# Pooled attention and a gated conv FFN on one core: conv on two blocks at once, keys of batches 2 to 7 in pairs

## The chip, the core and the metric

The kernel runs on one core of a Trainium2 chip. Its engines work side by side, each through its own list: TensorE (PE, matrix products; its weight loads are shown apart as PEld), VectorE (DVE), ScalarE (ACT), GpSimd (POOL) and SyncE (SP). Products land in PSUM, eight banks of 512 fp32 columns on 128 partitions. The metric is the device time of one execution in microseconds (us).

## The reference

Eight batches of 8 heads, 576 positions, 64 columns a head. Keys and values are averaged over groups of 8 positions (72 remain), softmax attention is computed against those 72, the heads are joined to x (8, 576, 512), and a gated FFN with a conv over positions follows. All inputs and outputs are fp32.

```python
k_p = k.reshape(B, H, Sp, pool, D).mean(axis=3)
v_p = v.reshape(B, H, Sp, pool, D).mean(axis=3)
scores = scale * np.matmul(q, k_p.transpose(0, 1, 3, 2))
attn = softmax(scores)                      # max subtracted first
x = join_heads(np.matmul(attn, v_p))
h = np.maximum(x @ w_in, 0.0)               # 512 -> 1024
conv_out = sum of conv_w[k] * h shifted by k - 1, k = 0..2
out = (h * sigmoid(conv_out)) @ w_out       # 1024 -> 512
```

## The kernel before

**Tiling.** Batches go in groups of two (g = 0 to 3). A group has nine query tiles of 128 rows (tile 4 takes 64 rows of each of its batches). The FFN works per batch on eight blocks `fb` of 128 hidden channels (partitions) by 576 positions, and writes out per tile of 128 rows.

**Keys, queries, values.** POOL loads all three with a cast to bf16 (`load_heads` L352, `load_v` L365). Keys of a batch are pooled on PE: `prep_k` (L464) multiplies each slice by the 0/1 matrix `pm`, which sums eight positions and turns the result at once, in two halves of 18 products with the array split in two (L469) or 36 with it split in four (L479); `copy_k` (L494) takes them out of PSUM. `prep_q` turns queries on PE (L533). `prep_v` adds values three times on DVE (L503, widths 1280, 640, 320) and multiplies them by the head mask into `vm` (L507), whose mask operand is broadcast along its last dimension. Key buffers: a ring `kp` of three, one a batch.

**Attention of a tile.** Scores on PE (L585), maximum on DVE (L598), subtraction (DVE L610 from group 1 on), exp on ACT (L636), a transpose of e (PE L647 in groups 0 and 1, then a DMA on SP's queue, L656), the product with `vm` (L672), division on DVE (L685, L687), and a transpose of x into `xT` (PE L704, or SP's DMA L696 in groups 2 and 3).

**FFN of a batch.** `ffn_in` (L717; batch 0 by tiles, L738) and a relu on ACT (L726) give `hT`. The conv is three products per position run with diagonal matrices `dw`, with the array split into four 64 by 64 parts: row half r, column half c. A part (r, c) with r = c reads `hT`; the parts with r different from c work on the same block with its two channel halves exchanged, which needs the copy `hX` (`ffn_swap`, L783, one DVE or ACT copy per half and pair of blocks). So one `ffn_conv` (L788) fills two banks of one block: row half r makes the positions of half r. Then tanh (ACT L815), plus one (DVE L825), times h (DVE L826) into `gT`, and `ffn_out` (L833, eight products of 512 columns a tile), a copy to `osb` (L844, ring of five) and two stores from SP's queue (L856).

**What sets the order.** `Graph.order` (L97) plans the whole program: every operation has a duration, the buffers it uses and a key (a due time plus a hand-set nudge). Among those that can start now, each engine takes the lowest key; PE's keys get `STAY` off if the array's split stays. `either` operations go to DVE or ACT. At most eight loads are in flight (L194). PSUM tokens take one bank or an aligned pair (`place`, L139). The list is then emitted in order of planned start, and each engine's list runs in that order. `first(name)` (L924) sets the keys of the early loads to -88 plus their place in `early` plus the nudge `('l', name)`.

Of the kernel before, what the change touches and what calls it, by code (L numbers as in the profile page):

```python
# [8 lines left out]
FP32 = mybir.dt.float32  # L9
# [24 lines left out]
class Graph:  # L34
# [8 lines left out]
    STAY = 111.55  # L43
    LAZY = 1.11
# [5 lines left out]
    ATT = 39.8  # L50
    SPREAD = -183.35
    PREP_K = -29.07
    PREP_Q = 51.67
    PREP_V = 749.64
    GATE = 126.95
    CONV = 47.63
    SWAP = 261.14
    QCONV = -325.78
    OUT = 297.24
    LAST = 982.97  # L60
    FIRST = 196.4
    V0 = 281.91
    DW = 1007.11
# [3 lines left out]
    SWAP_DVE = 8  # L67
    BANKS = 8
    URGENT = -857.49
    NUDGE = {  # L70
# [12 lines left out]
    }  # L83

    def __init__(self, rings):
        self.rings, self.ops, self.spares = rings, [], []

# [180 lines left out]
def kernel(  # L268
# [13 lines left out]
    POOL = 8  # L282
# [911 lines left out]
```

## Time and profile before

| What | us |
|---|---|
| median of three runs | 244.89 |
| the runs | 244.22, 244.89, 246.25 |
| span of the profiled execution | 244.0 |
| PE, DVE, ACT, POOL busy | 220.9, 182.0, 168.3, 29.1 |

The profiled execution is shown by its span, from its first to its last instruction; a clocked time of its own is not shown beside it. Its span lies 0.9 below the median and 0.2 below the shortest run.

A line of a group reads: source line, engine, operation, output <- inputs, shapes, count | busy us in total, mean ns of one | idle time of the engine just before, and what ended it. Matmuls are pipelined, so the duration of one is longer than the distance to the next. A line of waits reads: who waited <- for what: us in total, times, longest. In the table by stretch, each engine has its busy us and the number of its instructions in brackets; PEclk is the granted clock of PE as a share of full speed.

### The profile page before, as it was taken

How to read it: one execution, taken by the hardware profiler on the slowest of the kernel's cores; microseconds unless marked ns; L12 is line 12 of the kernel's file. 1: busy time of each engine (PE TensorE's matmuls, PEld its weight loads, DVE VectorE, ACT ScalarE, POOL GpSimd, SP SyncE). 2: the span in 40 equal slices, each digit the busy share in tenths (PEclk: the TensorE clock that was granted, in tenths of full speed). 3: DMA queues.
4: the chain of work that ended last, by engine and by line, in shares of the span. 5: the costliest groups of instructions: out<-in, count | busy, mean ns of one | idle time of the engine just before them, and what ended most of it. 6: DMA issues, size and time to landing. Idle time of an engine off the chain costs nothing.

```text
span 244.0 us, 7852 instructions
## 1 busy us (share of the span) xinstructions
PE 220.9 (91%) x3354; PEld 154.3 (63%) x3377; DVE 182.0 (75%) x398; ACT 168.3 (69%) x264; POOL 29.1 (12%) x48
## 2 busy tenths in 40 slices
PE   6568998998999999999999996979999999899991
PEld 2446986876675676678775554757655576676440
DVE  7667648899999999999999995755799413956301
ACT  2254764599996876498998654949966386989330
POOL 7942223200122020220010000000000000000000
PEclk9999999999999999999999999999999999999998
DMA  5999999999189958697208568593216577400356
GB/s 81 164 205 207 207 208 208 207 207 202 22 141 185 197 83 190 104 179 153 46 3 141 126 134 91 107 139 89 24 46 149 109 137 167 117 3 6 84 137 164
DMA packets 43707, 31.53 MB, mean 129 GB/s; under 512 B 23680, under 2 KB 39064, under 8 KB 43672
## 3 DMA queue, kind: packets, MB, share of 16 engines
q0 software_dynamic: 15952, 16.26, 42.2%
q1 hardware_dynamic: 27640, 14.64, 29.5%
q8 instruction: 26, 0.43, 0.7%
q10 hardware_dynamic: 80, 0.13, 0.2%
q14 instruction: 9, 0.07, 0.1%
HBM read 32.52 MB, written 9.44 MB: 172 GB/s over the span
## 4 chain that ended last, share of the span: by engine, by line
PE 51%; DVE 26%; ACT 8%; DMA 7%; issue 5%; POOL 0%; SPq 0%; DVEq 0%; ACTq 0%; POOLq 0%
PE psum L833 16%; PE psum L717 14%; PE psum L803 7%; DVE negm L598 5%; DVE gT L826 4%; PE psum L672 3%; DVE sd L610 3%; DMA kp<-in_k_dram 3%; PE psum L738 3%; DVE tg L825 2%; ACT hT L726 2%; DVE hX L783 2%; DVE x L687 2%; DVE v L503 2%; DMA eT<-e 2%
## 5 line engine op out<-in xcount | busy, mean ns | idle before, releaser
L833 PE MATMUL psum<-w_out_sb,gT 128*128 128x512 bf16 x266 | 66.6, 379 | 2.0 <-issue 0.8
L717 PE MATMUL psum<-xT,w_in_sb 128*128 128x288 bf16 x448 | 61.1, 286 | 2.0 <-DMA xT<-x 1.3
L717 PEld LDWEIGHTS <-w_in_sb 128*128 128x128 bf16 x448 | 41.8, 98 | 15.4 <-DMA xT<-x 1.6
L833 PEld LDWEIGHTS <-gT 128*128 128x128 bf16 x288 | 26.0, 98 | 25.9 <-issue 0.7
L815 ACT ACTIVATE tg<-psum 128x576 bf16<-128x576 f32 x64 | 37.8, 655 | 3.0 <-PE psum L803 2.5
L726 ACT ACTIVATE hT<-psum 128x576 bf16<-128x576 f32 x56 | 34.4, 648 | 7.5 <-PE psum L717 7.1
L844 ACT COPY osb<-psum 128x512 f32<-128x512 f32 (+1 forms) x31 | 17.9, 579 | 24.5 <-PE psum L833 23.3
L783 DVE COPY hX<-hT 64x1152 bf16<-64x1152 bf16 x41 | 18.7, 458 | 18.3 <-ACT hT L726 15.4
L803 PE MATMUL psum<-hT,dw 64*64 64x224 bf16 (+3 forms) x576 | 30.9, 246 | 0.8 <-ACT tg L815 0.7
L803 PEld LDWEIGHTS <-dw 64*64 64x64 bf16 x1152 | 24.7, 107 | 10.5 <-issue 9.5
L826 DVE TENSOR_TENSOR gT<-tg,hT 128x576 bf16<-128x576 bf16 x64 | 29.3, 458 | 2.2
L803 PE MATMUL psum<-hX,dw 64*64 64x288 bf16 (+3 forms) x576 | 30.7, 246 | 0.0
L598 DVE TENSOR_REDUCE negm<-psum 128x8 f32<-128x576 f32 (+1 forms) x36 | 25.9, 750 | 2.4 <-PE psum L585 2.2
L783 ACT COPY hX<-hT 64x1152 bf16<-64x1152 bf16 x23 | 26.4, 1150 | 0.5
L687 DVE TENSOR_TENSOR x<-psum,r 128x512 bf16<-128x512 f32 x36 | 24.9, 692 | 1.2
L636 ACT ACTIVATE e<-sd 128x576 bf16<-128x576 f32 x27 | 18.2, 682 | 8.1 <-DVE sd L610 6.7
L672 PE MATMUL psum<-vm,eT 128*128 128x130 bf16 (+5 forms) x240 | 18.5, 222 | 4.2 <-DMA eT<-e 2.2
L825 DVE TENSOR_SCALAR tg<-tg 128x576 bf16<-128x576 bf16 x64 | 19.4, 304 | 3.4 <-ACT tg L815 3.2
L672 PEld LDWEIGHTS <-eT 128*128 128x128 bf16 (+1 forms) x240 | 14.7, 100 | 9.4 <-issue 3.0
L610 DVE TENSOR_TENSOR sd<-psum,negm 128x576 f32<-128x576 f32 x27 | 19.6, 749 | 0.1
L685 DVE RECIPROCAL r<-psum 128x8 f32<-128x8 f32 x36 | 7.3, 201 | 8.8 <-PE psum L672 8.7
L543 ACT COPY qT<-psum 128x1152 bf16<-128x1152 bf16 (+2 forms) x11 | 10.7, 992 | 4.2 <-PE psum L533 4.1
(67 smaller groups left out, 227.9 us busy)
## 6 DMA issues: line engine op xcount, KB each, us to landing
out_dram<-osb SPq DMA_DIRECT2D x71, 128.0 KB, 2.4
v<-in_v_dram POOLq DMA_DIRECT2D x8, 512.0 KB, 8.8
kp<-in_k_dram POOLq DMA_DIRECT2D x7, 576.0 KB, 16.0
qp<-in_q_dram POOLq DMA_DIRECT2D x7, 576.0 KB, 12.5
w_in_sb<-in_moe_w_in_dram POOLq DMA_DIRECT2D x2, 512.0 KB, 14.7
w_out_sb<-in_moe_w_out_dram POOLq DMA_DIRECT2D x1, 1024.0 KB, 20.0
kp<-in_k_dram POOLq DMA_DIRECT2D x2, 288.0 KB, 5.4
v<-in_v_dram POOLq DMA_DIRECT2D x8, 64.0 KB, 8.4
```

Source lines behind the costliest of these rows:

```text
L598: nc.vector.tensor_reduce(out=a["m"][0:rows], in_=a["s"][0:rows, :, 0:2 * KW].rearrange("p a (h s) -> p a h s", s=Sp), axis=AX.X, op=OP.ma ...
L610: nc.vector.tensor_tensor(out=a["d"][0:rows], in0=a["s"][0:rows, :, 0:2 * KW].rearrange("p a (h s) -> p a h s", s=Sp), in1=a["m"][0:rows]. ...
L672: nc.tensor.matmul(out=a["o"][lo:hi, h // 4, (h % 4) * (D + 1):(h % 4 + x1 - x0) * (D + 1)], lhsT=a["eT"][:, j, lo:hi], rhs=buf("vm", b)[: ...
L687: nc.vector.tensor_tensor(out=a["x"][0:rows].rearrange("p (a h d) -> p a h d", a=2, d=D), in0=ov[:, :, :, 0:D], in1=r[0:rows].unsqueeze(3) ...
L717: nc.tensor.matmul(out=banks(ps)[:, j, 0:SC], lhsT=w_in_block(dc, fb), rhs=buf("xT", g)[:, dc, i * S + j * SC:i * S + (j + 1) * SC], start ...
L726: nc.scalar.activation(out=buf("hT", b)[:, fb, :].rearrange("p (a s) -> p a s", a=2), in_=banks(ps)[:, :, 0:SC], func=ACT.Relu, scale=0.5,)
L783: copy(out=buf("hX", b, f2)[r * D:(r + 1) * D, :, :], in_=buf("hT", b)[(1 - r) * D:(2 - r) * D, 2 * f2:2 * f2 + 2, :],)
L803: nc.tensor.matmul(out=cps[c * D:(c + 1) * D, r, lo:hi], lhsT=dw[r * D:(r + 1) * D, int(r != c), tap * n_fb + fb, :], rhs=hT[r * D:(r + 1) ...
L815: nc.scalar.activation(out=tg.rearrange("p (a s) -> p a s", a=2), in_=banks(ps)[:, :, 0:SC], func=ACT.Tanh, scale=0.5,)
L825: nc.vector.tensor_scalar(out=tg, in0=tg, scalar1=1.0, scalar2=None, op0=OP.add)
L826: nc.vector.tensor_tensor(out=buf("gT", g)[:, fb, i * S:(i + 1) * S], in0=tg, in1=buf("hT", b)[:, fb, :], op=OP.mult)
L833: nc.tensor.matmul(out=bank(ps)[0:rows, :], lhsT=buf("gT", g)[:, fb, t * P:t * P + rows], rhs=w_out_sb[:, fb, :], start=(fb == 0), stop=(f ...
```

## The change

Conv works on two neighbouring blocks in one operation. Part (r, c) takes block 2 f2 + (r xor c) straight from `hT`; so the odd block comes out with its channel halves exchanged, and each of the two blocks gets both position halves over two turns. `ffn_swap`, `hX` and the exchanged half of `dw` are gone; the operation takes two pairs of PSUM banks together. The gate of an odd block puts the halves back: two half-height additions of one, from `tg` into `gT`, then the product in place.

Keys of batches 0 and 1 are loaded and pooled as before, into halves of the one buffer `kk` (ring of 1). Those of 2 to 7 come in pairs of batches by one load, each partition holding 72 successive rows; DVE sums them in three additions (`pool_pair`, widths 2304, 1152, 576), PE only turns and sorts them with a selector `pick` (`turn_pair`, 18 products of 64 columns for both batches), and four copies (`copy_pair`) place them in `kT`.

The head mask is widened once into `mask_wide` and the `vm` product reads that. Output tiles of batches 3 to 6 are stored from POOL's queue, the others from SP's as before. The planner learns of two pairs of banks and of stores on POOL, and all keys and nudges are different numbers. The diff, cut to its core:

```diff
...
-    STAY = 111.55
-    LAZY = 1.11
+    STAY = 2433.79
+    LAZY = 9.06
...
+    KPOOL = 273.64
+    KTURN = 389.36
+    PREP_Q = 13123.61
+    CONV = -17463.4
+    QCONV = -11593.41
+    STORE_POOL = (3, 4, 5, 6)
+        ('kk', 1): 4004.89, ('kk', 2): -10943.52, ('kk', 3): 2758.46, ('l', 'ident'): 29827.78, ('l', 'k0'): -18933.08, ('l', 'k0+'): -1804.54,
+        ('l', 'k1'): 8531.98, ('l', 'kk1'): -15453.62, ('l', 'mask'): -5336.49, ('l', 'out'): 16585.15, ('l', 'pm'): 18123.21, ('l', 'q0'): -5392.93,
+        ('l', 'q0+'): -19585.27, ('l', 'q1'): -14428.56, ('l', 'q2'): -14105.83, ('l', 'q3'): -6312.58, ('l', 'v0'): 4052.12, ('l', 'v1'): 20762.22,
+        ('l', 'v2'): -6439.13, ('l', 'w0'): 11766.78, ('l', 'w1'): -7006.96, ('lk', 4): -8391.13, ('lk', 6): -8475.04, ('lq', 4): -6745.14,
...
-                f = place(need)
+                f = place(need) if need <= 2 else two_pairs()
...
+
+        def two_pairs():
+            f = [idle_from(x) for x in banks]
+            c = sorted(max(now, f[i], f[i + 1]) for i in range(0, len(f), 2) if None not in (f[i], f[i + 1]))
+            return c[1:2] or None
...
+                elif e == "POOL":
+                    o.end = max(wire, s + d + 0.3) + fixed
+                    landings += [o.end] * o.dmas
-             "hT": 2, "gT": 2, "xT": 2, "qT": 3, "kp": 3, "qp": 2, "hX": 3, "v": 2, "vm": 5, "kT": 5, "sd": 3, "r": 3, "s": 2}
+             "hT": 2, "gT": 2, "xT": 2, "qT": 3, "kk": 1, "qp": 2, "v": 2, "vm": 5, "kT": 5, "sd": 3, "r": 3, "s": 2}
...
+    mask_wide = const.tile([P, NJ, 3, D], BF16, name="mask_wide")
+    pick = const.tile([P, 2, D], BF16, name="pick")
-    cw_raw = const.tile([3 * n_fb, 3 * D], FP32, name="cw_raw")
-    convw = const.tile([P, 2, 3 * n_fb], FP32, name="convw")
+    cw_raw = const.tile([3 * n_fb, P], FP32, name="cw_raw")
+    convw = const.tile([P, 3 * n_fb], FP32, name="convw")
-    dw = const.tile([P, 2, 3 * n_fb, D], BF16, name="dw")
...
-        "hX": ([P, 2, S], BF16),
...
+    def k_rows_of(b):
+        t = buf("kk", 0).rearrange("p c x -> p (c x)")[:, b * H // 2 * S:(b + 1) * H // 2 * S]
+        return t.rearrange("p (h x) -> p h x", h=H // 2)
...
+    def load_pair(g):
+        rows = k[groups[g][0]:groups[g][1] + 1].rearrange("b h s d -> (b h s) d").rearrange("(p r) d -> p (r d)", p=P)
+        nc.gpsimd.dma_start(out=buf("kk", g).rearrange("p c x -> p (c x)"), in_=rows)
+
...
-        load_heads(buf("kp", b), k, b, **part)
+        load_heads(k_rows_of(b), k, b, **part)
...
-        nc.sync.dma_start(out=cw_raw[:, P:P + D], in_=cw[:, 0:D])
+        nc.sync.dma_start(out=cw_raw, in_=cw)
...
+    def widen_mask():
+        nc.vector.tensor_copy(out=mask_wide, in_=mask.unsqueeze(3).to_broadcast([P, NJ, 3, D]))
+
+    def build_pick():
+        for hh in range(2):
+            for f in range(2):
+                nc.vector.tensor_copy(
+                    out=pick[:, hh].rearrange("p (s f a e) -> p s f a e", s=2, f=2, a=2)[:, :, f],
+                    in_=ident.rearrange("p (s a hh f e) -> p s a hh f e", s=2, a=2, hh=2, f=2)[:, :, :, hh, f],
+                )
+
...
         nc.vector.tensor_tensor(
-            out=dw[:, x, todo],
+            out=dw[:, todo],
             in0=ident_2.unsqueeze(1).to_broadcast([P, n, D]),
-            in1=convw[:, x, todo].unsqueeze(2).to_broadcast([P, n, D]),
+            in1=convw[:, todo].unsqueeze(2).to_broadcast([P, n, D]),
             op=OP.mult,
...
+    def pool_pair(g, step):
+        t, half = buf("kk", g), POOL * D >> step + 1
+        nc.vector.tensor_tensor(out=t[:, :, 0:half], in0=t[:, :, 0:half], in1=t[:, :, half:2 * half], op=OP.add)
+
+    def turn_pair(g, ps):
+        flat = banks(ps).rearrange("p a x -> p (a x)")
+        for c in range(C):
+            for hh in range(2):
+                nc.tensor.matmul(
+                    out=flat[hh * D:(hh + 1) * D, c * D:(c + 1) * D],
+                    lhsT=buf("kk", g)[:, c, 0:D],
+                    rhs=pick[:, hh],
+                    start=True,
+                    stop=True,
+                    skip_group_check=True,
+                )
+
+    def copy_pair(b, ps, hh, copy):
+        g, i = where[b]
+        part = slice(hh * D, (hh + 1) * D)
+        src = banks(ps).rearrange("p a x -> p (a x)")[part, 0:C * D].rearrange("p (c s j e) -> p s j e c", s=2, j=4, e=8)
+        copy(
+            out=buf("kT", b)[part, :, hh * Sp:(hh + 1) * Sp].rearrange("p j (e c) -> p j e c", c=C),
+            in_=src[:, i],
+        )
...
             in0=vt[:, :, 0:D].unsqueeze(2).to_broadcast([P, NJ, 3, D]),
-            in1=mask.unsqueeze(3).to_broadcast([P, NJ, 3, D]),
...
-    def ffn_swap(b, f2, r, copy):
-        copy(
-            out=buf("hX", b, f2)[r * D:(r + 1) * D, :, :],
-            in_=buf("hT", b)[(1 - r) * D:(2 - r) * D, 2 * f2:2 * f2 + 2, :],
-        )
-    def ffn_conv(b, fb, ps):
+    def ffn_conv(b, f2, pss):
         g, i = where[b]
-        hT, hX = buf("hT", b), buf("hX", b, fb // 2)
-        cps = banks(ps)
-        for n in range(max(map(len, todo))):
-            for r in range(2):
-                for c in range(2):
-                    if n >= len(todo[r]):
+        for turn in range(2):
+            for n in range(max(map(len, todo))):
+                for r in range(2):
+                    j = r ^ turn
+                    if n >= len(todo[j]):
                         continue
-                    tap, lo, hi, src = todo[r][n]
-                    nc.tensor.matmul(
-                        out=cps[c * D:(c + 1) * D, r, lo:hi],
-                        lhsT=dw[r * D:(r + 1) * D, int(r != c), tap * n_fb + fb, :],
-                        rhs=hT[r * D:(r + 1) * D, fb, src:src + hi - lo] if r == c
-                        else hX[r * D:(r + 1) * D, fb % 2, src:src + hi - lo],
-                        start=(n == 0),
-                        stop=(n == len(todo[r]) - 1),
-                        skip_group_check=True,
-                    )
+                    tap, lo, hi, src = todo[j][n]
+                    for c in range(2):
+                        fb = 2 * f2 + (r ^ c)
+                        nc.tensor.matmul(
+                            out=banks(pss[r ^ c])[c * D:(c + 1) * D, j, lo:hi],
+                            lhsT=dw[r * D:(r + 1) * D, tap * n_fb + fb, :],
+                            rhs=hT[r * D:(r + 1) * D, fb, src:src + hi - lo],
+                            start=(n == 0),
+                            stop=(n == len(todo[j]) - 1),
+                            skip_group_check=True,
+                        )
 
-            out=buf("gT", g)[:, fb, i * S:(i + 1) * S], in0=tg, in1=buf("hT", b)[:, fb, :], op=OP.mult
-        )
+        tg, gate = buf("tg", b, fb), buf("gT", g)[:, fb, i * S:(i + 1) * S]
+        if fb % 2:
+            for r in range(2):
+                nc.vector.tensor_scalar(
+                    out=gate[r * D:(r + 1) * D], in0=tg[(1 - r) * D:(2 - r) * D], scalar1=1.0, scalar2=None, op0=OP.add
+                )
+            tg = gate
+        else:
+            nc.vector.tensor_scalar(out=tg, in0=tg, scalar1=1.0, scalar2=None, op0=OP.add)
+        nc.vector.tensor_tensor(out=gate, in0=tg, in1=buf("hT", b)[:, fb, :], op=OP.mult)
...
+        if kind == "k":
+            toks[b] = kk.setdefault(0, tokens.get(("kk", 0)) or token("kk", 0))
...
+    def add_load_pair(g, key):
+        kk[g] = token("kk", g)
+        loads["kk", g] = add({"POOL": 0.65}, key, lambda: load_pair(g), uses=[kk[g]], land=(LATE, 2 * kb, RATE))
...
+    def add_pair(g, key):
+        b0 = groups[g][0]
+        prev = None
+        for step, d in enumerate((1.352, 0.752, 0.452)):
+            prev = add(dve(d), key + nudge("kk", g) + Graph.KPOOL + step, lambda step=step: pool_pair(g, step),
+                       after=[prev, loads["kk", g]], uses=[kk[g]])
+        t = token("ps", n=2)
+        for b in groups[g]:
+            ktok[b], kdone[b] = token("kT", b), []
+        o = add({"PE": 0.30}, key + nudge("kk", g) + Graph.KTURN, lambda: turn_pair(g, t), after=[prev, picked],
+                uses=[t, kk[g]], mode=HALF, count=36)
+        for b in groups[g]:
+            for hh in range(2):
+                c = add(either(0.46, 0.42), key + nudge("kk", g) + Graph.KTURN + 1, None, after=[o, zk], uses=[t, ktok[b]])
+                c.emit = lambda c=c, b=b, hh=hh: copy_pair(b, t, hh, copier(c))
+                kdone[b].append(c)
+
...
-        for step, d in enumerate((0.81, 0.49, 0.32, 1.16)):
+        for step, d in enumerate((0.81, 0.49, 0.32, 0.65)):
...
+        for f2 in range(n_fb // 2):
+            fbs = (2 * f2, 2 * f2 + 1)
+            cbs, tgs = [token("ps", n=2) for _ in fbs], [token("tg", b, fb) for fb in fbs]
+            conv = add({"PE": 0.66}, w + 6 * f2 + Graph.QCONV, lambda f2=f2, cbs=cbs: ffn_conv(b, f2, cbs),
+                       after=relu[fbs[0]] + relu[fbs[1]] + dwo, uses=cbs + tgs + [htok[b], gtok[g]], mode=QUARTER, count=64 + 12 * i)
...
-            add({"SP": 1.18}, key, lambda t=t: ffn_store(g, t, nc.sync), after=[o], uses=[osb], land=(2.0, 0, 1))
+            if b in Graph.STORE_POOL:
+                add({"POOL": 1.55}, key, lambda t=t: ffn_store(g, t, nc.gpsimd), after=[o], uses=[osb], land=(2.4, 0, 1)).dmas = 2
+            else:
+                add({"SP": 1.18}, key, lambda t=t: ffn_store(g, t, nc.sync), after=[o], uses=[osb], land=(2.0, 0, 1))
...
```

More of the change, by code (lines that the diff above doesn't have):

```diff
@@ L49 @@
     IN_FLIGHT = 8
[L50 to L63, printed above, removed]
+    ATT = -1794.24
+    SPREAD = -4830.66
+    PREP_K = -4885.51
+    KPOOL = 273.64
+    KTURN = 389.36
+    PREP_Q = 13123.61
+    PREP_V = 12374.2
+    GATE = 153.55
+    CONV = -17463.4
+    QCONV = -11593.41
+    OUT = 10943.62
+    LAST = 8939.04
+    FIRST = 17466.52
+    V0 = -17959.82
+    DW = 14591.19
     X_DMA = 4
@@ L466, in prep_k @@
             for hh in range(2):
-                k_rows = buf("kp", b)[:, 2 * half + hh, c * D:(c + 1) * D]
+                k_rows = k_rows_of(b)[:, 2 * half + hh, c * D:(c + 1) * D]
                 if mode == HALF:
@@ L929 @@
     add_load("k", 0, first("k0+"), 0.5, heads=slice(2, 4))
-    cwl = add({"SP": 1.1}, soon(), load_conv, land=(1.5, 0, 1))
+    cwl = add({"SP": 0.6}, soon(), load_conv, land=(1.5, 0, 1))
     cb0 = add({"DVE": 0.25}, soon(), lambda: nc.vector.memset(blank, 0.0))
@@ L1009, in add_prep_v @@
         prev = None
-        for step, d in enumerate((0.81, 0.49, 0.32, 1.16)):
+        for step, d in enumerate((0.81, 0.49, 0.32, 0.65)):
             prev = add(dve(d), key + step * gap, lambda step=step: prep_v(b, step),
-                       after=[prev, lv[b], hmc], behind=[vdone.get(b - 1)], uses=[vtok[b]] + [vmtok[b]] * (step == 3))
+                       after=[prev, lv[b], hmc, hmw], behind=[vdone.get(b - 1)], uses=[vtok[b]] + [vmtok[b]] * (step == 3))
         vdone[b] = prev
```

89 lines of the change are left out of this document (41 added, 48 removed), and 21 rows, old and new, of the table NUDGE.

## The prediction

> **What bounds the kernel now.** The page first, for the span and the share of each engine; then the chain that ended last.
>
> ```profile
> span 244.0 us, 7852 instructions
> PE 220.9 (91%) x3354; PEld 154.3 (63%) x3377; DVE 182.0 (75%) x398; ACT 168.3 (69%) x264; POOL 29.1 (12%) x48
> PE 51%; DVE 26%; ACT 8%; DMA 7%; issue 5%; POOL 0%; SPq 0%; DVEq 0%; ACTq 0%; POOLq 0%
> ```
>
> TensorE (PE) carries half of the chain, VectorE (DVE) a quarter. Those are averages, so next the table of busy time by stretch:
>
> ```profile
> core 0: us, PE busy (x) PEld busy (x) DVE busy (x) ACT busy (x) POOL busy (x), PEclk, DMA share, GB/s
> 0.00:24.00 24.00, 16.07 (x225) 10.27 (x228) 17.27 (x46) 9.36 (x18) 14.55 (x27) 1.00 1.05 163
> 24.00:48.00 24.00, 22.75 (x473) 20.27 (x468) 16.79 (x34) 14.84 (x22) 6.33 (x9) 1.00 1.23 208
> 48.00:96.00 48.00, 45.63 (x866) 33.19 (x869) 46.58 (x99) 39.52 (x64) 4.82 (x7) 1.00 0.88 156
> 96.00:144.00 48.00, 46.67 (x680) 32.45 (x685) 46.20 (x94) 38.49 (x60) 3.40 (x5) 1.00 0.63 109
> 144.00:168.00 24.00, 20.50 (x247) 14.78 (x246) 14.75 (x34) 15.81 (x26) 0.00 (x0) 1.00 0.73 121
> 168.00:228.00 60.00, 58.38 (x835) 38.59 (x842) 39.28 (x93) 46.99 (x72) 0.00 (x0) 1.00 0.40 81
> 228.00:244.00 16.00, 10.92 (x50) 4.80 (x49) 1.12 (x2) 3.30 (x6) 0.00 (x0) 0.94 0.54 131
> ```
>
> From 48 to 144 us DVE (92.8 of 96) and PE (92.3) are both full; from 168 to 228 PE alone (58.4 of 60). From 24 to 228 us PE stands idle for only 204 - 193.9 = 10.1 us, a third of it in 144 to 168. The granted clock is 1.00 throughout, so no clock gain is open. The gain is therefore limited by what PE no longer has to do, plus part of these 10.1 us. Two of PE's waits there, from the list of waits, and the queue of SyncE (SP) just before, from the timeline:
>
> ```profile
> PE psum L672 <- DMA eT<-e: 2.2, 1, 2.2
> PE psum L717 <- DMA xT<-x: 1.3, 1, 1.3
> ```
>
> ```profile
> 159.38 2.98 SPq L856 DMA_DIRECT2D out_dram<-osb  x4
> 162.45 1.26 SPq L696 DMA_TRANSPOSE xT<-x  x1
> 163.76 2.51 SPq L856 DMA_DIRECT2D out_dram<-osb  x4
> ```
>
> Stores and DMA transposes share SP's queue; a transpose waits behind 3 us of store issues. The prices come from the groups by line and shape:
>
> ```profile
> L826 DVE TENSOR_TENSOR gT<-tg,hT 128x576 bf16<-128x576 bf16 x64 | 29.3, 458 | 2.2
> L783 ACT COPY hX<-hT 64x1152 bf16<-64x1152 bf16 x23 | 26.4, 1150 | 0.5
> L825 DVE TENSOR_SCALAR tg<-tg 128x576 bf16<-128x576 bf16 x64 | 19.4, 304 | 3.4 <-ACT tg L815 3.2
> L783 DVE COPY hX<-hT 64x1152 bf16<-64x1152 bf16 x41 | 18.7, 458 | 18.3 <-ACT hT L726 15.4 <-PE psum L803 2.0
> L507 DVE TENSOR_TENSOR vm<-v,mask 128x960 bf16<-128x960 bf16 x8 | 9.2, 1156 | 0.2
> L469 PE MATMUL psum<-pm,kp 128*64 128x144 bf16 x180 | 8.2, 247 | 3.6 <-DMA kp<-in_k_dram 3.6
> L503 DVE TENSOR_TENSOR v<-v 128x1280 bf16<-128x1280 bf16 x8 | 6.5, 818 | 0.2 <-DMA v<-in_v_dram 0.2
> L503 DVE TENSOR_TENSOR v<-v 128x640 bf16<-128x640 bf16 x8 | 3.9, 489 | 0.2
> L479 PE MATMUL psum<-pm,kp 64*64 64x72 bf16 x216 | 3.0, 197 | 0.0
> ```
>
> **Keys on PE.** The pooling products of batches 2 to 7 go. Restricted to lines 469 and 479, the stretches 20 to 96 us show 1.51 + 4.06 + 1.12 + 1.01 = 7.7 us busy in 12 half-batches. A run's last matmul shows about 0.2 us that the next run overlaps, so 7.7 - 12 x 0.2 = 5.3 leaves the path. Three groups of 18 products over 64 columns are added; the nearest row, 18 transposes of 128 columns (line 533), lasts 0.69 us, so at most 2.1, and half of that by columns. I take 0.8: net -4.5, ends -3.2 (5.3 - 2.1) and -6.7 (7.7 - 1.0). PE is full there, so all of it counts.
>
> **Keys on DVE.** The two rows of line 503 give (818 - 489)/640 = 0.514 ns an element, so 2304, 1152 and 576 elements take 1.34 + 0.75 + 0.46 = 2.55 us a pair, 7.7 us for three. Two pairs fall in 48 to 144. The copies out of PSUM keep their number (12 of 288 elements a partition, 0.39 us on ScalarE (ACT), 0.45 on DVE) and read with a stride: from no change to double, of which I take no change, since one element takes about 1 ns in the other PSUM reads too (692 ns for 512); doubled it is 12 x 0.4 = 5 us on ACT, which has 18 us free in 48 to 144.
>
> **Conv.** Two blocks hold as many products and weight loads as before (two old blocks in a row, 218.44 to 219.39 us, take 0.95 us). A change of tile shape costs 0.11 to 0.14 us at each end; I count 29 separate conv runs now and there can be about 32, so nothing. The copies of h go: 26.4 us of ACT, 18.7 of DVE. Every odd block gets a second half-height addition: 32 x 0.30 = +9.7 us of DVE (between 0.15 and 0.30 each; a 64-partition copy pays by its columns, so the upper end).
>
> **vm product.** Eight at 1.156 us. At the slope of line 503, 960 elements would take 0.65: between 0 and -4.0 us of DVE, and I take -4.0. The Trainium skill, VectorE: DVE Perf Modes, section What auto-detection actually checks, asks 16-bit operands with step one for two results a cycle; the old mask operand stands still along its last dimension, the new one does not, so by the page -4.0. Left at 1.156, DVE keeps 3 us more in 48 to 144, which still does not pass PE, and the total stays.
>
> **DVE and ACT together, 48 to 144 us.** DVE 92.8 - 10.2 (22 hX copies) + 4.9 (16 additions) - 3.0 (six vm) + 5.1 (two key pairs) = 89.6; ACT 78.0 - 11.5 (ten hX copies) = 66.5. ACT can then take half of the 6.6 us of qT, eT and xT copies that DVE makes there: DVE 86. PE: 92.3 less its share of the keys = 89. PE is then the fuller one and this stage can end 3 us earlier by its work alone; that is inside the -4.5.
>
> **Waits.** Of the 10.1 us I take 4: 2 of 3.5 in 144 to 168 (no hX copy between relu and conv, 0.46 to 1.15 us each, and fewer stores in SP's way), 1.5 of 3.7 in 48 to 144, 0.5 elsewhere. Ends: 0 and 10.1.
>
> **Stores.** 18 tiles of batches 3 to 6, 36 issues, leave SP (0.587 each, 21 us) for GpSimd (POOL; a load issue there takes 0.55 to 0.77, so 27 us). POOL is busy 29 us, none after 128. Its queue also holds the loads of batches 4 to 7, which wait up to 18.5 us for a buffer (q7, issued 126.8); a store ordered behind such a load waits too. SP's 14th tile, the first of batch 3 if stored in order, is issued at about 160, so at nothing.
>
> **Start.** The nudges order POOL's loads by key, lowest first: second part of q0, first half of k0, q1, second half of w_in, first part of q0, rest of k0, v0, k1; pm and ident follow only when eight transfers are in flight. So 2.3 MB, counted in bf16, instead of 0.85 MB land before the first scores. At the rates of slices 1 to 3 (81, 164, 205 GB/s) that is about 16 us instead of 11, and v0 19 instead of 13. But k0, both q0, v0, k1, q1 and the weights are the same 5.05 MB, landed at about 29 us in both orders, and PE can turn q1 meanwhile. I take +1.5, ends 0 and +5. One key buffer instead of three: the pair of 2 and 3 can be loaded once batch 1 is pooled (now 20 us), and batch 2 is now pooled at 38 to 41; the median landing of 16 us just fits, at nothing. If it is late, the +5 covers it. The smaller conv tables take two 0.95 us products from DVE, the widened mask and the selector add 0.3 to 1.6, while DVE waits for the first scores: nothing.
>
> **Sum.** 244.0 - 4.5 - 4 + 1.5 = 237.0 us of span. The profiled span is 0.9 below the median of 244.89, so 237.9.
>
> **Rivals.**
> Everything recovered: all 10.1 us, nothing lost at the start. 244.0 - 4.5 - 10.1 + 0.9 = 230.3. Against it: PE and DVE stay within 3 us of each other for 96 us.
> No gain: DVE stays the bound. If ACT takes no copies, vm stays at 1.156 and all three pairs are pooled after 48 us, DVE holds 89.6 + 3.0 + 2.5 = 95.1, above the 92.8 of now; the 2.3 us more and the late start's +1.5 meet the 2 + 0.5 us of waits and 1.4 of keys outside this stage: about 244.8. Against it: ACT has 29 us free there.
> Slower: a conv now needs four of the eight PSUM banks at once and holds the second pair through two tanh (0.24 + 2 x 0.655 us). PE works through one list, in the order planned, so a wait for banks stops it whole. Each of the 32 convs has 7/32 = 0.22 us to lose before the gain is gone. A wait of one tanh (0.655) at every second gives 16 x 0.655 = 10.5: 248.4. For it: the only bank wait of a conv now (0.7 us, on a tanh) already stands in a stretch of four blocks in a row. Against it: tanh starts earlier, ACT being rid of the hX copies.
> Late stores: five output buffers, 1.73 us of PE per tile. A store then costs 1.5 to issue and, at the median landing of v's load, 8.8, plus 0.6 of copy: 10.9/5 = 2.2 us a tile, 0.45 too much, 18 x 0.45 = 8 us: 246. It decides above a landing of 5 x 1.73 - 2.1 = 6.5 us; loads' landings include the queue of other loads, and SP's stores land in 2.4. The Trainium skill, SBUF, State Buffer, section Who interferes with whom, says that GpSimd cannot write descriptors while DVE runs a two-port operation. No slowing shows here: load issues at 66 to 108 us, with DVE full, take the same 0.74 to 0.77 us as at 4 us.
>
> **Chances.** Forecast 0.60 (233 to 242); everything recovered 0.16; no gain 0.08; conv waits for banks 0.11; late stores 0.05. About 1% is what a measurement of this kernel can tell from no change. Faster 0.76 (the first two), same 0.09 (no gain, a little of late stores), slower 0.15. Range 229.5 to 245.5: from all waits recovered and the larger end of the keys, to no gain; the slower cases, 0.14, lie mostly outside.
>
> **What would show it.** Right: no hX; lines 469 and 479 only before about 25 us; odd blocks' additions at 0.30; DVE clearly below PE from 48 to 144; vm at 0.65; store issues on POOL with landings under 6.5 us. Wrong: PE waiting for tanh ahead of conv, copies of osb waiting for stores, first scores later than 17 us without being made up by 48, or strided key copies far above 0.45.

## The result, and the profile after

The changed kernel takes 252.22 us (median of 250.58, 251.78, 252.66 and 252.88); the kernel before, on the same chip, 245.56 (244.22, 244.89, 246.22, 246.25). Ratio 1.029, interval 1.023 to 1.035: slower by about 3%, where 237.9 us and a gain were forecast. The profiled execution of the changed kernel has a span of 248.9 us; its own time, 250.58, is 1.7 more. It is the fastest of the four, so the trace shows 4.9 us of the 6.7 that the medians lie apart. Spans are compared with spans below. Medians and ratios leave out executions over 1.5% above the fastest of the same kernel (one of run 2, two of run 11).

The page of the changed kernel, the lines that answer to those of before:

```profile
span 248.9 us, 7483 instructions
PE 217.9 (88%) x3172; PEld 149.5 (60%) x3194; DVE 175.7 (71%) x396; ACT 148.2 (60%) x246; POOL 45.2 (18%) x81
PE 44%; DVE 26%; issue 10%; DMA 9%; POOL 5%; ACT 5%; DVEq 0%; ACTq 0%; POOLq 0%; SPq 0%
```

PE, DVE and ACT each work less than before: PE by 3.0 us, DVE by 6.3, ACT by 20.1. The span is 4.9 us longer all the same, so PE must stand idle 7.9 us more. The table by stretch shows where:

```profile
core 0: us, PE busy (x) PEld busy (x) DVE busy (x) ACT busy (x) POOL busy (x), PEclk, DMA share, GB/s
0.00:24.00 24.00, 14.45 (x168) 9.14 (x169) 16.15 (x47) 8.52 (x14) 13.88 (x26) 0.86 1.07 170
24.00:48.00 24.00, 22.74 (x489) 20.34 (x489) 18.15 (x38) 15.90 (x24) 3.87 (x6) 1.00 1.19 209
48.00:96.00 48.00, 45.02 (x651) 30.62 (x650) 44.61 (x93) 37.43 (x65) 6.44 (x10) 1.00 0.88 165
96.00:144.00 48.00, 43.51 (x699) 30.41 (x704) 44.45 (x97) 31.12 (x52) 4.11 (x7) 1.00 0.48 90
144.00:168.00 24.00, 18.91 (x205) 13.03 (x204) 13.27 (x28) 10.00 (x17) 2.17 (x5) 0.86 0.82 138
168.00:228.00 60.00, 57.19 (x838) 38.36 (x846) 32.78 (x81) 37.09 (x63) 9.75 (x19) 1.00 0.37 70
228.00:244.00 16.00, 15.89 (x144) 7.61 (x144) 5.83 (x16) 7.79 (x14) 4.95 (x10) 1.00 0.51 123
```

From 24 to 228 us PE is idle for 204 - 187.4 = 16.6 us (10.1 before), 4.5 in 96 to 144 and 5.1 in 144 to 168. In 144 to 168 the granted clock falls to 0.86 as well, and PE's busy time grows for the same work: the 448 `ffn_in` products of line 766 are busy for 62.8 us in all, those of line 717 before for 61.1. The waits of PE name two kinds of transfer and one addition:

```profile
PE psum L582 <- POOL ident masks.py:199: 5.7, 1, 5.7
PE psum L721 <- DMA eT<-e: 4.0, 4, 1.3
PE psum L766 <- DMA xT<-x: 3.1, 2, 2.6
PE psum L530 <- DVE kk L524: 2.1, 2, 1.6
```

The first line is at the start. The next two are SP's transposes by DMA, 7.1 us together; before, 2.2 + 1.3. In the changed kernel L705 and L745 issue them, L905 the stores. SP's queue in the timeline of the changed kernel at that time (start, duration of the issues):

```profile
140.52 1.22 SPq L745 DMA_TRANSPOSE xT<-x  x1
141.84 1.30 SPq L705 DMA_TRANSPOSE eT<-e  x1
143.23 5.64 SPq L745 DMA_TRANSPOSE xT<-x  x2
148.97 5.08 SPq L705 DMA_TRANSPOSE eT<-e  x3
```

And POOL's, with the idle time ahead of an issue and what ended it:

```profile
140.20 0.77 POOL L369 DMA_DIRECT2D qp<-in_q_dram  x1 [32.88 <-PE psum L582]
141.83 2.26 POOL L905 DMA_DIRECT2D out_dram<-osb  x4 [0.86 <-ACT osb L893]
147.03 2.08 POOL L905 DMA_DIRECT2D out_dram<-osb  x4 [2.94 <-DVE osb L893]
```

POOL waited 32.9 us for a q buffer (the queries of batch 6, loaded ahead of those of 5, are turned only at 135 to 140), then sent batch 7's q and, right behind it, eight stores of batch 3. Before, that load left at 126.8 and was in at 134, and SP issued no store from 143.1 to 159.4. Now two issues of transposes take 5.64 us instead of 2 x 1.22. The DMA part for 142 to 150 us shows the packets (queue 0 is GpSimd's, queue 1 SP's; then issues, KB each, and median us to landing):

```profile
q0 software_dynamic: 645, 0.95, 76.6%
q1 hardware_dynamic: 1096, 0.27, 34.7%
...
out_dram<-osb POOLq DMA_DIRECT2D x8, 128.0 KB, 7.4
eT<-e SPq DMA_TRANSPOSE x2, 8.0
xT<-x SPq DMA_TRANSPOSE x2, 8.6
```

GpSimd's packets hold 77% of the sixteen engines, and a transpose takes 8 us to land, not the 2.5 to 2.6 that was the median before.

The prices of the new operations came out as they were forecast (L543 is a copy out of PSUM):

```profile
L871 DVE TENSOR_SCALAR gT<-tg 64x576 bf16<-64x576 bf16 x64 | 19.6, 306 | 1.2
L556 DVE TENSOR_TENSOR vm<-v,mask_wide 128x960 bf16<-128x960 bf16 x8 | 5.2, 653 | 0.1
L524 DVE TENSOR_TENSOR kk<-kk 128x2304 bf16<-128x2304 bf16 x3 | 4.1, 1354 | 1.9 <-DMA kk<-in_k_dram 1.9
L524 DVE TENSOR_TENSOR kk<-kk 128x1152 bf16<-128x1152 bf16 x3 | 2.2, 750 | 0.0
L543 DVE CAST kT<-psum 64x288 bf16<-64x288 f32 x4 | 1.8, 460 | 0.6 <-ACT kT L543 0.5
L524 DVE TENSOR_TENSOR kk<-kk 128x576 bf16<-128x576 bf16 x3 | 1.3, 450 | 0.0
```

### The profile page after: what moved, and what is told of

The parts are those of the page before. It is cut to its first block, busy times and chain, and to the rows that moved or that the text cites. A ratio compares the mean times of both kernels' runs of the same rounds, so it can differ in the third digit from the quotient of the medians.

```text
span 248.9 us, 7483 instructions
## 1 busy us (share of the span) xinstructions
PE 217.9 (88%) x3172; PEld 149.5 (60%) x3194; DVE 175.7 (71%) x396; ACT 148.2 (60%) x246; POOL 45.2 (18%) x81
## 4 chain that ended last, share of the span: by engine, by line
PE 44%; DVE 26%; issue 10%; DMA 9%; POOL 5%; ACT 5%; DVEq 0%; ACTq 0%; POOLq 0%; SPq 0%
PE psum L766 15%; PE psum L882 12%; PE psum L848 7%; DMA eT<-e 4%; DVE gT L877 4%; DVE negm L647 4%; DVE gT L871 3%; PE psum L787 3%; DVE x L736 3%; PE psum L721 3%; DVE sd L659 3%; DMA v<-in_v_dram 3%; ACT tg L859 2%; DMA xT<-x 2%; DVE v L552 2%
## 5 line engine op out<-in xcount | busy, mean ns | idle before, releaser
L766 PE MATMUL psum<-xT,w_in_sb 128*128 128x288 bf16 x448 | 62.8, 290 | 3.3 <-DMA xT<-x 3.1
L775 ACT ACTIVATE hT<-psum 128x576 bf16<-128x576 f32 x56 | 35.3, 651 | 23.9 <-PE psum L766 23.8
L859 ACT ACTIVATE tg<-psum 128x576 bf16<-128x576 f32 x64 | 38.0, 649 | 14.0 <-PE psum L848 10.1
L905 POOL DMA_DIRECT2D out_dram<-osb x36 | 18.9, 532 | 77.8 <-ACT osb L893 74.8
L848 PE MATMUL psum<-hT,dw 64*64 64x288 bf16 (+4 forms) x1152 | 30.5, 246 | 0.1
L848 PEld LDWEIGHTS <-dw 64*64 64x64 bf16 x1152 | 24.4, 107 | 10.2 <-issue 9.5
L876 DVE TENSOR_SCALAR tg<-tg 128x576 bf16<-128x576 bf16 x32 | 9.9, 308 | 27.8 <-ACT tg L859 27.8
L871 DVE TENSOR_SCALAR gT<-tg 64x576 bf16<-64x576 bf16 x64 | 19.6, 306 | 1.2
L877 DVE TENSOR_TENSOR gT<-tg,hT 128x576 bf16<-128x576 bf16 x32 | 14.7, 458 | 1.1
L877 DVE TENSOR_TENSOR gT<-gT,hT 128x576 bf16<-128x576 bf16 x32 | 14.6, 458 | 1.1
L634 PE MATMUL psum<-kT,qT 128*128 128x144 bf16 (+1 forms) x140 | 12.6, 226 | 2.8 <-DVE kT L543 1.3
L369 POOL DMA_DIRECT2D qp<-in_q_dram x9 | 7.0, 782 | 41.1 <-PE psum L582 38.5
## 6 DMA issues: line engine op xcount, KB each, us to landing
kk<-in_k_dram POOLq DMA_DIRECT2D x3, 1152.0 KB, 11.2
```

The lines of the kernel that those rows point to most:

```text
L766: nc.tensor.matmul(out=banks(ps)[:, j, 0:SC], lhsT=w_in_block(dc, fb), rhs=buf("xT", g)[:, dc, i * S + j * SC:i * S + (j + 1) * SC], start ...
L775: nc.scalar.activation(out=buf("hT", b)[:, fb, :].rearrange("p (a s) -> p a s", a=2), in_=banks(ps)[:, :, 0:SC], func=ACT.Relu, scale=0.5,)
L848: nc.tensor.matmul(out=banks(pss[r ^ c])[c * D:(c + 1) * D, j, lo:hi], lhsT=dw[r * D:(r + 1) * D, tap * n_fb + fb, :], rhs=hT[r * D:(r + 1 ...
L859: nc.scalar.activation(out=tg.rearrange("p (a s) -> p a s", a=2), in_=banks(ps)[:, :, 0:SC], func=ACT.Tanh, scale=0.5,)
L871: nc.vector.tensor_scalar(out=gate[r * D:(r + 1) * D], in0=tg[(1 - r) * D:(2 - r) * D], scalar1=1.0, scalar2=None, op0=OP.add)
L877: nc.vector.tensor_tensor(out=gate, in0=tg, in1=buf("hT", b)[:, fb, :], op=OP.mult)
```

## The experiments

The theory at first was that transfers collide: three places where a load or a store of GpSimd's meets something that PE waits for. Its rivals were that stores on GpSimd's queue are bad by themselves, and that the new order of the program is bad whatever runs beside it. Runs 1 to 4, 5 to 8 and 9 to 12 each share a chip and runs of the kernel before, whose medians are 244.79, 244.75 and 244.80 us. In all but runs 7 and 8 PE runs the changed kernel's products in the changed kernel's order, so that the start of one and the same product can be compared between runs. A ring that is made larger gives an operation another buffer, not another place in the order. "Interval" below is the time from the first `ffn_in` product of batch 4 to the first of batch 5: 19.9 us in the changed kernel (146.5 to 166.4).

**1. Stores back on SP, order kept.**

```diff
-                add({"POOL": 1.55}, key, lambda t=t: ffn_store(g, t, nc.gpsimd), after=[o], uses=[osb], land=(2.4, 0, 1)).dmas = 2
+                add({"POOL": 1.55}, key, lambda t=t: ffn_store(g, t, nc.sync), after=[o], uses=[osb], land=(2.4, 0, 1)).dmas = 2
```

> Same planned order as the changed kernel; only the queue of the 18 stores of batches 3 to 6 differs (SP again, at the same places). Theory C (a load and stores on GpSimd's DMA queue slow the transposes of 143 to 158 us by sharing the DMA engines, and the load of q7 is the larger half): about 2 of the 6.7 us come back, 250 us. Rival S (the stores from GpSimd are the cause alone): 245 us. Rival P (the planned order itself is slow, DMA has no part): no change, 252.

Measured: 250.51 us, ratio to before 1.022 (1.015 to 1.029). The median landing of a transpose is back at 2.6 and 2.5 us, yet the interval is 20.2 us and PE's wait for e has grown from 4.0 us:

```profile
PE psum L721 <- DMA eT<-e: 7.7, 5, 2.1
```

The time is the 250 of theory C, but the median over the whole program hides where the loss lies. Batch 7's q load still leaves from GpSimd, at 141.6, and the transposes beside it still land late. The DMA part from 142 to 150 us:

```profile
xT<-x SPq DMA_TRANSPOSE x3, 6.7
eT<-e SPq DMA_TRANSPOSE x1, 8.9
```

SP moreover issues eight stores, of 0.47 to 0.96 us each, between the transposes from 144.9 to 157, so that later ones go out late. The run refutes rival S (245): with the stores off GpSimd nearly all of the loss is still there. It can't tell what SP's queue costs by itself.

**2 and 3. A third q buffer; a second key buffer.** In each, the ring is larger (`{'kk': 2}` in run 3) and the slots are dealt out anew after planning; the order stays.

```diff
+    MORE = {'qp': 3}
...
+        for ring, n in self.MORE.items():
+            for i, k in enumerate(taken[ring]):
+                k.slots = [i % n]
```

> Same planned order; a third buffer for queries, so the load of q7 no longer waits for the turning of q5 and can be issued about 107 us instead of 140. Theory C: the transposes of 143 to 158 us run at their usual 2.6 us while q7 is out of the way, 5 us come back, 247. Rival S: no change, 252. Rival P: 252.

> Same planned order; two key-pair buffers, so the loads of the pairs 4,5 and 6,7 go out some 12 us earlier. Theory K (one key buffer chains turn, load, sum, and the last pair lands 2 to 3 us late at 95 us): the stretch 94 to 101 us loses its wait, 2.5 us come back, 249.7. Rival P: 252.

Measured: 252.93 us (1.028, 1.019 to 1.038) and 251.14 (1.026, 1.019 to 1.032), so neither gain came. The q load of run 2 now left at 108 us, into the transposes of e of batch 4, which land in up to 10.2 us there, and the loss moved with it; the eight stores still met the later ones (interval 17.9). In run 3 the wait of 1.6 us for the last key pair was gone, and what it gave was lost again in the transposes at 143 to 150.

**4. All three together,** the edits of runs 1, 2 and 3.

> The three edits together, same planned order. Theories C and K: the losses add up to about 10 us, so 241 to 243 us, below the kernel before; this would be what the change in arithmetic is worth without the collisions. Rival P: still above 250.

Measured: 250.67 us (1.024, 1.017 to 1.030). The gains did not add up. The interval is 19.5 us, and PE's wait for e is the longest of all runs:

```profile
PE psum L725 <- DMA eT<-e: 10.9, 6, 3.1
```

4.0 of it falls before 125 us, where the q load, now issued at 106.3, meets the transposes of batch 4 as in run 2, and 5.8 between 125 and 170. In that second stretch no load of GpSimd's is left: from 142 to 150 us the transposes land in medians of 2.4 and 2.6 us, but they share SP's queue with eight stores and go out late. The theory in its additive form fell. What was left of it: the transposes must have both the DMA engines and SP's queue to themselves, and none of these four runs gave them both. That is T below, against P: the order is at fault.

**5. Nothing beside the transposes.** Two things are left out: the load of batch 7's q and eight stores. (The buffer that batch 7's q is turned from then holds rows of batch 6, not of batch 5 as the text has it.)

> The changed kernel in its own order of issue, with two things left out: the load of batch 7's q (so its turn works on the rows of batch 5 that lie in that buffer) and the GpSimd stores of the first four tiles of batch 3. Part of the output is therefore not computed or not stored; the run prices the traffic. Theory T (traffic): the changed kernel loses about 8 us between 143 and 150 because GpSimd's transfers run beside the transposes by DMA, which then land in 6 to 10 us; without them they land in 2.4 to 2.7 us, PE keeps the planned order there, and the time falls from 252.2 by 7 to 9.5 us, to 243 to 245. Theory P (order): the planned order, with SP's transposes back to back from 130 to 157, is too tight on the chip whatever runs beside it; the landings shorten but the time stays at 249 to 252.

Measured: 245.71 us, ratio 1.003 (1.000 to 1.006); interval 13.6 us in place of 19.9. That is a little above T's 243 to 245, and far below P's 249. P is refuted: the same order, with no buffer added and less this traffic, takes 6.5 us less.

**6. The same traffic at other times.** Nothing is left out. A one-element copy on POOL reads a landed transpose and so holds its queue until then.

```diff
+    MORE = {'qp': 3, 'osb': 9}
...
         for o in graph.order():
+            if o in moved:
+                continue
             o.emit()
+            for g, t in late:          # (2, 0): q of batch 7; (3, 1): eight stores of batch 3
+                if o is xdone[g, t]:
+                    nc.gpsimd.tensor_copy(out=held[0:1, 0:1], in_=buf("xT", g)[0:1, 0, t * P:t * P + 1])
+                    for x in late[g, t]:
+                        x.emit()
```

> The changed kernel with everything computed and the same transfers, but at other times: the load of batch 7's q goes out as soon as the last transpose of x of batch 4's first four tiles has landed (about 119 us; a third q buffer makes that free), and the GpSimd stores of batch 3's first four tiles go out when the transpose of x of tile 1 of batch 6 has landed (about 160 us; nine output buffers in place of five). The order on every other engine is unchanged. Theory T: as without the traffic, to within 1.5 us: 243 to 246, and transposes between 137 and 158 land in 2.4 to 2.7 us. Theory P: 249 to 252. If the stores only carry their collision to a later place (transposes of x at 160 to 170 and of e at 174), 246 to 249 with the lag back by 180.

Measured: 246.37 us, 1.002 (0.997 to 1.007); interval 13.9. The load left at 123.4, the stores at 166.3. Of the eleven transposes issued from 137 to 158 us whose landing the trace has, nine took 2.4 to 2.6 us and two 4.1 and 4.3. The whole computation and the same bytes, 5.8 us faster, by when they move: T, though 0.4 above its range. The number also fits the last case of the expectation, a collision carried to a later place, but its sign is missing: the first `ffn_in` product of batch 6 starts at 192.2 us here and at 196.5 in the changed kernel, so the lag is not back.

**7. Stores on SP, order planned anew.**

```diff
-    STORE_POOL = (3, 4, 5, 6)
+    STORE_POOL = ()
```

> The changed kernel with the stores of batches 3 to 6 back on SP and the order planned anew for that (planned end 236.2 us against 235.1 of the changed kernel), not the frozen order with SP's issues pushed in, as in the first run. The new plan interleaves three of the stores with the transposes. Theory T: batch 7's q load (planned at 137 to 143) still lands beside the transposes and SP has no slack: 247 to 250. Theory P (it was the order): the order that knows of SP's load holds its plan like the kernel before did (+2.9 us): 240 to 242.

Measured: 249.46 us, 1.020 (1.017 to 1.023). A plan that knows of SP's load does not save it. Over the whole program its transposes land in medians of 2.6 and 2.5 us, but batch 7's q load leaves at 141.3, and the transposes issued from 141.6 to 149.8 us take 4.0 to 8.6 to land. That is the collision that T named; P's 240 to 242 is wrong for the order that this planner finds.

**8. The kernel before with the stores of batches 3 to 6 from GpSimd.**

```diff
-            add({"SP": 1.18}, key, lambda t=t: ffn_store(g, t, nc.sync), after=[o], uses=[osb], land=(2.0, 0, 1))
+            add({"SP": 1.18}, key, lambda t=t: ffn_store(g, t, nc.gpsimd if 3 <= b <= 6 else nc.sync), after=[o], uses=[osb], land=(2.0, 0, 1))
```

> The kernel before, in its own order, with one part of the change: the stores of batches 3 to 6 go from GpSimd's queue. In it SP's stores lie at 133 to 138, 145 and 159 to 167, mostly behind the transposes. From GpSimd they go as soon as their tile is copied. Theory T: some of them then run beside the transposes by DMA at 140 to 160, which land in more than 4 us there: 247 to 250. Theory P, and any theory that puts the loss on batch 7's q load alone: 244 to 246, since the order is unchanged and SP is relieved of 1.2 us a tile.

Measured: 247.45 us, 1.011 (1.009 to 1.012). Nothing but the queue of 36 stores has changed. The transposes of the old kernel land later, as T says. The DMA part of this run (number of issues, median us to landing; 2.6 and 2.5 without the edit):

```profile
eT<-e SPq DMA_TRANSPOSE x18, 4.2
xT<-x SPq DMA_TRANSPOSE x18, 3.5
```

So this part of the change is a loss by itself, of 2.7 us between medians, in an order that has no q load beside the transposes. But the time is in T's range by luck: the trace doesn't show T's mechanism. PE waits for e no longer than the 2.2 us of before, its interval is 14.9 us (16.6), and its last product ends at 238.6 us (239.0). What grew is the end, from PE's last product to the end of the span: 6.7 us in place of 5.0. In the old order the last stores are tiles of batch 6, which now leave from GpSimd, the last at 240.2. GpSimd's closing DRAIN starts at 240.1 and takes 4.43 us, to 244.6; the engines finish behind it. (The second line below is of the view by source line: count, shortest/median/longest ns, first and last start.)

```profile
PE psum L672 <- DMA eT<-e: 2.1, 3, 1.2
L1189 POOLq DRAIN  x3: 51/93/4434, 240.1 to 245.1; - x3
```

So 1.7 us of the loss stands at the end of the program; the other microsecond is in neither trace. In this order the later landings cost PE nothing that the trace shows. In the changed kernel the same DRAIN starts at 237.0 and is over before SP's last stores land, and the end takes 4.6 us.

**9 and 10. The halves of run 6:** only batch 7's q moved, only the stores moved.

> One half of the run with both moved (246.4 us): only the load of batch 7's q is moved, to after the last transpose of x of batch 4's first tiles (it went at 123 us there); batch 3's stores stay where the changed kernel has them, beside the transposes. Theory T: the eight stores alone, 2 to 3 us of transfer, keep some landings at 4 to 7 us: about half of the loss, 248 to 250. If the load alone was at fault: 245.5 to 247. If the stores alone were: 251 to 253.

> The other half: batch 3's stores of four tiles are held until the transpose of x of tile 1 of batch 6 has landed; batch 7's q load stays at 140 us, beside the transposes. Theory T: the load's 1.2 MB alone delays those that are issued in its 6 us, and the planned lag of 3.5 us is passed by 2 to 4: 248 to 250. If the load alone was at fault: 251 to 253. If the stores alone were: 245.5 to 247.

Measured: 248.67 us (1.015, 1.007 to 1.022) and 249.15 (1.016, 1.010 to 1.022), both in the range of T and not in those of a single culprit (single executions scatter from 247.5 to 251.1). The intervals are 17.2 and 15.7: beside 13.9 with neither, the stores alone cost 3.3 there and the load alone 1.8, of 6.0 together. By medians it is 2.3 and 2.8, of 5.8, so which of the two costs more stays open.

**11. The eight stores from ScalarE's queue.** Batch 7's q moved as in run 9.

```diff
-                st = add({"POOL": 1.55}, key, lambda t=t: ffn_store(g, t, nc.gpsimd), after=[o], uses=[osb], land=(2.4, 0, 1))
+                st = add({"POOL": 1.55}, key, lambda t=t: ffn_store(g, t, nc.scalar if b == 3 and t < 8 else nc.gpsimd), after=[o], uses=[osb], land=(2.4, 0, 1))
```

> As the run with only batch 7's q load moved, but the eight stores of batch 3's four tiles are issued from ScalarE's queue in place of GpSimd's, at the same places in the order, beside the same transposes. It tells whether it is GpSimd's queue or any store beside them. If GpSimd's queue is at fault (each of its stores holds the transposes up): transposes at 140 to 158 land in 2.4 to 3 us and the time is 246 to 248, ScalarE paying 8 issues of 0.6 us. If any transfer beside them does it: landings as with GpSimd's stores, 248 to 251.

Measured: 247.28 us, 1.011 (1.007 to 1.015). This answer is mixed. The transposes issued from 143 to 151 us land in 3.7 to 5.5 us, so a store from another queue holds them up as well, nearly as GpSimd's do (4.8 to 5.75 in run 9). Yet PE lost less: the interval is 13.7 us, as in run 6 (13.9) and not as in run 9 (17.2), with one wait of 1.0 us for x ahead of it. The time lies 1.4 us under run 9's and 0.9 above run 6's, neither clear of the scatter. So landings of up to 5.5 us cost PE little here, and whether that is the queue or the few tenths by which the issues lie differently stays open.

**12. Everything quiet.** As run 6, with batch 7's v held back as well (and its four DVE operations put at 149 to 167 us), two key buffers, and five output buffers as in the changed kernel.

```diff
+    MORE = {'qp': 3, 'kk': 2}
...
+            late[2, 0] = loads["q", b] + [lv[b]]
```

> The changed kernel with its whole computation and with all the loads and the stores of batch 3 moved off the transposes: batch 7's q and v loads after the last transpose of x of batch 4's first tiles (with it, batch 7's pooling of v moves to four places at 149 to 167), batch 3's stores after tile 1 of batch 6, and two key buffers, so that the last key pair doesn't wait for its buffer. Theory T: the run with q and stores moved had a span of 245.3; the last key pair's wait (1.4 us) and the transposes of e beside batch 7's v (0.6 to 1.2) come back: span 242.5 to 243.5, time 244 to 245.5. Theory P: nothing more than there, 246 to 247. If the earlier key load collides with others as it did in the run with two key buffers alone: 246 to 248.

Measured: 244.13 us, 0.996 (0.993 to 0.999), span 241.3: the fastest of all, 3.2% under the changed kernel and just under the kernel before. The profiled execution is the fastest of ten (243.04). SP's queue of it:

```profile
138.72 1.22 SPq L750 DMA_TRANSPOSE xT<-x  x1
140.03 1.22 SPq L710 DMA_TRANSPOSE eT<-e  x1
141.34 3.25 SPq L750 DMA_TRANSPOSE xT<-x  x2
144.69 3.95 SPq L710 DMA_TRANSPOSE eT<-e  x3
148.70 5.64 SPq L750 DMA_TRANSPOSE xT<-x  x4
```

Four transposes of x in the 5.64 us that two took. Its DMA part from 142 to 150 us has no packet of GpSimd's:

```profile
q1 hardware_dynamic: 3178, 0.77, 59.3%
...
xT<-x SPq DMA_TRANSPOSE x3, 3.2
eT<-e SPq DMA_TRANSPOSE x3, 2.6
```

3178 packets of SP's queue in eight microseconds, against 1096 in the changed kernel. And its table by stretch, for the comparison below:

```profile
0.00:24.00 24.00, 15.27 (x163) 9.60 (x164) 15.56 (x46) 8.00 (x14) 13.88 (x26) 0.86 1.07 171
24.00:48.00 24.00, 22.51 (x466) 20.02 (x467) 18.21 (x39) 15.93 (x24) 3.90 (x6) 1.00 1.19 209
48.00:96.00 48.00, 45.58 (x682) 30.92 (x669) 46.48 (x96) 37.38 (x64) 6.49 (x10) 1.00 0.88 170
96.00:144.00 48.00, 45.72 (x716) 31.34 (x715) 43.14 (x94) 31.86 (x54) 2.26 (x4) 1.00 0.52 101
144.00:168.00 24.00, 22.25 (x339) 17.03 (x337) 17.16 (x40) 15.34 (x27) 4.46 (x9) 1.00 0.57 100
168.00:228.00 60.00, 57.83 (x808) 36.26 (x806) 34.55 (x84) 36.19 (x61) 12.61 (x24) 1.00 0.43 85
```

## Why the prediction was wrong, step by step

The spans split into PE's busy and idle time (from the tables by stretch, that of run 8 included; "after 228" is span less 228 less busy there):

| us | before | changed | run 8 | run 12 |
|---|---|---|---|---|
| PE busy | 220.9 | 217.9 | 222.9 | 217.9 |
| idle, 0 to 24 | 7.9 | 9.6 | 7.0 | 8.7 |
| idle, 24 to 228 | 10.1 | 16.6 | 8.7 | 10.1 |
| idle, after 228 | 5.1 | 4.8 | 6.7 | 4.6 |
| span | 244.0 | 248.9 | 245.3 | 241.3 |

The traces of before and of the changed kernel lack records of PE: 3354 products beside 3377 weight loads, and 3172 beside 3194. A product that is missing shows as less busy time and more idle time. Runs 8 and 12 have a product for every weight load, and run 8 is the old kernel but for the queue of its stores, so the terms of the forecast that concern PE are best read between these two.

**The step that failed: "Stores ... at nothing".** The issues were priced (36 of 0.53 us on POOL, forecast 0.55 to 0.77) and what waits behind them, but not what runs beside them. The prediction asked of each transfer whose queue it waits in; it never asked what a store or a load does to the transposes that share the sixteen DMA engines and that PE waits for. With all stores on SP, as in runs 1, 4 and 7 and in the kernel before, a transpose's median landing over the program is 2.5 to 2.6 us, and SP issues the two one after the other; from another queue the stores run beside them. In the changed order run 9 prices the eight stores of batch 3 at 2.3 us above run 6, run 10 prices batch 7's q load at 2.8, and both together, the changed kernel, lie 5.8 above it. The load belongs to the same step: the text quoted its issue at 126.8 and said that a store behind it would wait, and did not ask where the load itself would go. It went to 140.2, since its q buffer came free later. The price hangs on the order: in the old one (run 8) landings of 4.2 us cost PE nothing that the trace shows. There the stores cost 1.7 us at the end of the program, which the prediction did not ask about either.

**Waits, forecast -4.** This is the second step that failed, and it failed with the traffic out of the way too. In 144 to 168, where 2 of 3.5 us were forecast to come back, run 12 has 1.75 left, nearly as forecast. Over the rest of 24 to 228 its idle time is 8.4 us, and 6.6 at most before. In sum run 12 stands idle 10.1 us there and run 8 only 8.7: 1.4 more, not 4 less. The old order had two large gaps, 2.2 and 1.3 us, beside six of 0.3 to 0.9. The two are gone, and run 12 has fourteen of 0.3 to 1.2 us, on e, `kT`, x and others. In the changed kernel it is 6.5 us worse, which is the step above and the next.

**One key buffer, "just fits at nothing".** The pair that came last (batches 4 and 5) was issued at 83.6, when the buffer was free, landed 11.2 us later, and PE waited 1.6 us for its sums; the prediction had looked at the pair of 2 and 3 alone. In run 12, with two buffers, the same wait is 0.5, and from batch 2's first `ffn_in` product to batch 3's it takes 15.2 us (92.9 to 108.1) instead of 17.0 (92.4 to 109.4). In run 3, with two buffers and nothing else changed, it is 15.2 as well (93.5 to 108.7). The term was some 1.8 us, not nothing.

**Keys on PE, -4.5.** Right, as far as the traces tell. Between runs 8 and 12 PE's busy time falls by 5.0. (Between the traces of before and of the changed kernel it falls by 3.0, but the changed kernel's clock of 0.86 in 144 to 168 adds to the second.) By rows the pooling fell from 11.1 us (8.15 + 2.96) to 4.4 (2.0 and 1.0 for batches 0 and 1, and 1.4 for three turns of 0.47). At the start the granted clock was 0.86 instead of 1.00 and more fill products ran (15; 12 before, 13 in run 8), which adds to the busy time; the parts can't be told apart in the trace.

**Start, +1.5.** First scores at 17.8 us (12.2 before), PE idle 1.6 us more until 24, and a quarter of all `ffn_in` products are through at 45.1 (48.5 before): as forecast, and by that count made up, though the order is another. Between runs 8 and 12 PE's idle time until 24 grows by 1.7.

**DVE, ACT, conv, vm, copies.** Right: 306 ns for the half additions (0.30), 1.35 + 0.75 + 0.45 us a pair (2.55), 0.65 for vm, so the trace agrees with what the prediction took from the Trainium skill, VectorE: DVE Perf Modes, section What auto-detection actually checks (653 ns). The copies out of PSUM cost 0.39 on ACT and 0.46 on DVE, as much as without the stride before (0.39 and 0.45).

**The rivals.** No conv waited for a bank: the longest wait of PE for a tanh is 0.2 us. The rival "late stores" had the right suspect and the wrong mechanism. Landings of 7.4 us did pass its limit of 6.5 from 142 to 150, but no copy waited for an output buffer; the transposes did the waiting. From run 8 to run 12 the span splits into 245.3 - 5.0 (work) + 1.7 (start) + 1.4 (waits) - 2.1 (end, 1.7 of which is run 8's own) = 241.3. That is bookkeeping and proves no cause, but it shows which terms held: work and start did, and the waits came out 5.4 us the other way. The trace of run 12 is of its fastest execution; by medians it is only 0.7 us under the kernel before.

Left open: why the waits grew in run 12 outside of 144 to 168. Stores of batches 4 and 5 still run beside the transposes of 183 to 190 us there, of which four land in 4.4 to 5.9 us, and PE waits 1.1 us for e there; that was not tried apart.

## What to carry to other kernels

When a transfer moves to another queue, list what it will then run beside: a queue that two kinds of transfer share also issues them one after the other. If PE waits for DMA transposes and the order leaves no slack, give their stretch to them alone, both the DMA engines (no load, no store) and the issuing queue; here that was worth 5.8 us of 252 with no instruction saved. Where the order has slack, a late landing costs nothing (run 8): look where in the trace the time went before you give a cause for it, also when the time is the one that you expected. Look at the program's last stores too. A one-element copy that reads a landed tile is enough to hold a queue back until then.

## What the runs showed of the hardware

Five transposes (four of e, one of x) that run alone in run 12 move 0.79 MB in 3232 packets, 244 bytes each; the packets of GpSimd's that they met from 142 to 150 us in the changed kernel average 0.95 MB / 645 = 1.5 KB. Beside these, landings went from 2.6 to 8.0 us for e and from 2.5 to 8.6 for x. The issue on SP lengthens too: 1.22 us alone, 2.8 each when the transposes ahead had not landed. From 144 to 168 us the granted clock fell to 0.86 in the changed kernel, where PE was busy for 18.9 of 24 us, and stayed at 1.00 in run 12 with 22.3.
